# Attention output transposed straight into its packed tile, items taken in pairs, and a new planned order, in a one-core transformer block on Trainium2

## The chip, the core and the metric

The kernel runs on one core of one Trainium2 chip. The time is the device time of the whole program in microseconds; three runs of the kernel before took 803.64, 804.56 and 806.51 us, median 804.56. Profiles come from one profiled execution each.

## What is computed

The reference is one adaLN-conditioned transformer block on `x` of 2048 rows by 640 columns, in bfloat16:

```python
mod = (_silu(c) @ w_mod).reshape(c.shape[0], 6, 1, -1)      # sa, ca, ga, sb, cb, gb
h = _layernorm(x, axis=-1) * (1 + ca) + sa
x = x + ga * _A_ref(h, A_wqkv, A_wo)    # 32 heads of width 20, softmax over all 2048 keys
h = _layernorm(x, axis=-1) * (1 + cb) + sb
x = x + gb * _B_ref(h, B_w_gate, B_w_up, B_w_down)          # (h @ gate) * (h @ up) @ down, width 1536
```

## The kernel before

**The work.** The queries are cut into seven chunks (`CHUNKS`): one of 512 and six of 256. The 32 heads are eight groups of four; the four heads of a group sit in the four 32-row strips of a tile. A chunk and a group make an **item** (57 of them; the last of the last chunk is cut into two halves of 128 queries). Each item is cut into **units**: 512 columns of scores of one head in one PSUM bank (one block of 128 keys by 512 queries, or two by 256). There are 2048 units.

**Two ways to the exponential.** Most units go to ScalarE, two units, 1024 columns, to one exponential (`fexp`, line 1561) into a ring `PP` of eight double slots. The rest go to VectorE in **quads** of four units: it reads the scores from PSUM as integers (`fp1`, line 1585) and makes two terms by bit operations (lines 1617 and 1625) and one product, on POOL in four pieces (line 1637) or on VectorE (line 1622). `QUADS` says how many quads each item has, 107 in all: 428 units by VectorE, 1620 by ScalarE in 810 exponentials. A quad's units are multiplied with V twice, once for each term.

**The order.** `build_kernel` makes `Task` objects with durations, dependencies, priorities and buffers (`Slots`), and `Sched` plays them on a model of the engines; the order that comes out is written as five fixed instruction streams (`emit_program`, line 356). TensorE's next piece is chosen in `pick_pe` (line 2396): scores first when ScalarE has a bank free (`setA` and `setB`, two banks each), score work for VectorE attached to them (`d_attach`, line 2351), then products with V (`pv_issue`, line 2207), then pieces of projections and of the second half of the block (`pick_x`, line 2294). Constants such as `SEM`, `PE_DRAIN`, `ACT_LAT` and a table `STAGE` for each item set delays and thresholds. On SP's queue the transfers are taken by priority as soon as they are ready in the model.

**The end of an item** (`item_end_tasks`, line 1707). The products with V of one item gather in one bank of the pool `G` (four banks), 21 rows per head: a row of sums and 20 of output. Then VectorE transposes 32x32 blocks into `OT` (`t1`, line 1717), takes reciprocals of the sums (`t2`, line 1723), the normalisation goes to POOL or, for the last item of a chunk, to VectorE (`f3`, line 1725), and VectorE transposes back into `OcT` (`t4`, line 1734). Now each head's 20 rows stand in a strip of 32, and DMAs on SP's queue copy them to packed rows of `Ocp`, four or five for an item (line 1746):

```python
return e.dma_start(Ocp[r0:r0 + nr, slot, b5, qo:qo + n],
                   OcT[32 * s + 1 + ro:32 * s + 1 + ro + nr, cell["s"], 0:n])
```

The very last group has no copy; its `OcT` is multiplied directly with `wo7`, a small spread copy of the last rows of w_o.

**The second half** of a chunk (`suffix`, line 1773) runs beside the attention of the next chunk: out-projection from `Ocp` and `wo_sb` (`qf(320, ...)`), layernorm, transposes, gate and up with weights staged by DMA into `stg` (three buffers), a product (lines 1959 and 1966 for chunks of 256, one block of 128 hidden columns at a time, gate and up side by side in one bank), down-projection, and the output DMA (line 2071). The second half of the last chunk is the tail of the kernel. Early on the same SP queue carries the round trip of K and Q through DRAM (`packed_round`, line 1224: writes at line 1276, reads at 1289 and 1298).

## Time and profile before

| what | value |
|---|---|
| median of three runs | 804.56 us |
| span of the profiled execution | 803.8 us |
| first exponential starts, last ends | 16.35 us, 775.87 us |
| VectorE, ScalarE, TensorE busy, 16 to 109 us | 76.24, 85.71, 90.75 of 93 us |
| the same, 109 to 776 us | 595.30, 665.17, 661.40 of 667 us |
| the same, 776 to 804 us | 15.53, 4.05, 24.92 of 28 us |
| issues of copies from `OcT` to `Ocp` on SP | 248, median 714 ns |

How to read the lines below: a group's row has the source line, the engine, the operation, output and input with their shapes, the count after x, then busy time and mean duration, then the idle time ahead of it with what ended it. A row of the timeline has start, length, engine, line and count of instructions run together. In a table of windows each engine has its busy time and, in brackets, its count; behind them stand TensorE's granted clock, the share of DMA and GB/s. A waits row has total, times and longest. PEld is TensorE's weight load, which carries the wait of the matmul behind it; SPq is SP's DMA queue.

### The profile page before, as it was taken

The page shows a single profiled execution, that of the slowest core. Times are in us where ns is not written, and L with a number is a line of the kernel's source. Part 1 is how long each engine was busy: PE and PEld are TensorE (multiplying, and loading weights), DVE is VectorE, ACT ScalarE, POOL GpSimd, SP SyncE. Part 2 cuts the span into 40 slices and gives each one's busy share as a digit, 9 for nine tenths or more (in the row PEclk, how much of TensorE's full clock was granted, in tenths as well). Part 3 has the DMA queues.
Part 4 walks back from the last instruction along what each step waited for, and adds up shares of the span by engine and source line. Part 5 has one row for each costly group of instructions (what it writes and reads, how often), then busy time and mean ns, then how long its engine had stood idle before and what let it go on. Part 6 is the DMA issues. An engine that isn't in the chain of part 4 may idle for free.

```text
span 803.8 us, 37761 instructions
## 1 busy us (share of the span) xinstructions
PE 790.4 (98%) x16595; PEld 380.6 (47%) x16595; DVE 697.8 (87%) x1401; ACT 764.8 (95%) x847; POOL 386.0 (48%) x396
## 2 busy tenths in 40 slices
PE   8999999999999999999999999999999999999998
PEld 4433433333244434445555455555555555555567
DVE  7978788799989999988999999999899988898754
ACT  6899899999999999999999999999999999999961
POOL 3347455654366565763444443545534554455300
PEclk9999999999999999999999999999999999999999
DMA  9733212212341532120032404231540254414420
GB/s 297 243 113 91 62 43 64 61 33 76 92 109 50 167 88 52 35 55 13 24 81 65 95 16 112 57 73 39 121 89 15 54 118 94 98 37 106 92 68 18
DMA packets 154314, 64.66 MB, mean 80 GB/s; under 512 B 116951, under 2 KB 154151, under 8 KB 154151
## 3 DMA queue, kind: packets, MB, share of 16 engines
q1 hardware_dynamic: 153223, 61.10, 30.0%
q8 instruction: 132, 2.16, 1.1%
q10 hardware_dynamic: 928, 1.15, 0.5%
q14 instruction: 31, 0.25, 0.1%
HBM read 50.63 MB, written 8.99 MB: 74 GB/s over the span
## 4 chain that ended last, share of the span: by engine, by line
PE 77%; ACT 14%; DVE 5%; issue 2%; DMA 1%; SPq 1%; POOL 0%; DVEq 0%; ACTq 0%
PE ps_all L1524 26%; PE ps_all L970 21%; PE ps_all L2192 19%; ACT PP L1561 14%; PE ps_all L1230 4%; PE ps_all L966 3%; DVE DB L1585 2%; PE ps_all L1889 1%; PE ps_all L1166 1%; PE ps_all L1127 1%; DVE DSS L1617 1%; PE ps_all L2523 0%; DVE DSS L1625 0%; DMA QT<-q_rows 0%; PE ps_all L991 0%
## 5 line engine op out<-in xcount | busy, mean ns | idle before, releaser
L1561 ACT ACTIVATE PP<-ps_all 128x1024 bf16<-128x1024 f32 x810 | 748.5, 1090 | 6.7 <-PE ps_all L1524 4.8
L1637 POOL TENSOR_TENSOR DSS<-DB,DSS 128x512 bf16<-128x512 bf16 x268 | 305.0, 1157 | 290.6 <-DVE DSS L1625 254.2
L1585 DVE TENSOR_SCALAR DB<-ps_all 128x512 int16<-128x512 f32 x428 | 285.5, 681 | 50.5 <-PE ps_all L1524 48.0
L1524 PE MATMUL ps_all<-QT,KT 32*128 32x256 bf16 (+2 forms) x3648 | 319.4, 287 | 4.5 <-DMA QT<-q_rows 0.8
L1524 PEld LDWEIGHTS ps_all<-QT,KT 32*128 32x128 bf16 x3648 | 93.9, 92 | 204.1 <-ACT PP L1561 141.5
L2192 PE MATMUL ps_all<-PP,Vf 128*32 128x256 bf16 (+2 forms) x2892 | 163.6, 291 | 0.5 <-DVE KPB L1242 0.3
L970 PE MATMUL ps_all<-h2T,stg 128*32 128x256 bf16 (+2 forms) x2716 | 122.9, 281 | 0.3 <-DVE DB L1585 0.2
L2192 PEld LDWEIGHTS ps_all<-PP,Vf 128*32 128x32 bf16 (+1 forms) x2892 | 54.5, 94 | 76.4 <-issue 67.6
L2192 PE MATMUL ps_all<-DSS,Vf 128*32 128x256 bf16 (+1 forms) x1512 | 88.7, 291 | 0.0
L1617 DVE TENSOR_SCALAR DSS<-DB 128x2048 int16<-128x2048 int16 x107 | 77.2, 722 | 0.8
L970 PEld LDWEIGHTS ps_all<-h2T,stg 128*32 128x32 bf16 x2716 | 61.6, 96 | 26.9 <-issue 22.0
L1625 DVE TENSOR_SCALAR DSS<-DB 128x2048 int16<-128x2048 int16 x107 | 73.2, 684 | 0.8 <-PE ps_all L2192 0.8
L970 PE MATMUL ps_all<-wd,hprod 128*32 128x320 bf16 (+1 forms) x1404 | 61.0, 277 | 0.0
L1725 POOL TENSOR_TENSOR OTn<-OT,invT 128x256 bf16<-128x256 f32 (+1 forms) x49 | 35.3, 721 | 37.7 <-DVE invT L1723 37.5
L1622 DVE TENSOR_TENSOR DSS<-DB,DSS 128x2048 bf16<-128x2048 bf16 x40 | 51.5, 1287 | 0.0
L2192 PEld LDWEIGHTS ps_all<-DSS,Vf 128*32 128x32 bf16 x1512 | 36.5, 95 | 20.9 <-issue 12.4
L970 PE MATMUL ps_all<-wV,hT 128*32 128x160 bf16 x1280 | 38.9, 236 | 0.9 <-DVE DB L1585 0.3
L970 PEld LDWEIGHTS ps_all<-wd,hprod 128*32 128x32 bf16 x1404 | 31.2, 96 | 14.2 <-issue 10.8
L1717 DVE STREAM_TRANSPOSE OT<-ps_all 128x256 f32<-128x256 f32 (+2 forms) x57 | 27.1, 475 | 8.8 <-PE ps_all L2192 8.5
L1230 PE MATMUL ps_all<-hT,wk 128*32 128x512 bf16 x360 | 32.3, 382 | 0.0
L970 PEld LDWEIGHTS ps_all<-wV,hT 128*32 128x32 bf16 x1280 | 24.6, 97 | 15.9 <-issue 8.2
L1230 PE MATMUL ps_all<-hT,wq 128*32 128x512 bf16 x375 | 31.3, 382 | 0.6 <-DVE OT L1717 0.6
(133 smaller groups left out, 556.1 us busy)
## 6 DMA issues: line engine op xcount, KB each, us to landing
stg<-in_B_w_gate_dram SPq DMA_DIRECT2D x74, 160.0 KB
stg<-in_B_w_up_dram SPq DMA_DIRECT2D x74, 160.0 KB
KT<-k_rows SPq DMA_DIRECT2D x112, 32.0 KB
QT<-q_rows SPq DMA_DIRECT2D x48, 64.0 KB
Ocp<-OcT SPq DMA_DIRECT2D x164, 10.0 KB
wm<-in_w_mod_dram SPq DMA_DIRECT2D x3, 800.0 KB
x<-in_A_x_dram SPq DMA_DIRECT2D x7, 320.0 KB
k_rows<-KPA SPq DMA_DIRECT2D x16, 128.0 KB
```

Of the source, the lines that this page charges most:

```text
L970: return lambda e, b: e.matmul(ps[32 * x:32 * x + 32, b, c0 + o:c0 + o + w], lhs()[:, 32 * x:32 * x + 32], rhs() if w == n else rhs()[:, o ...
L1230: f = [lambda e, b_, k=k, x=x: e.matmul(ps[x:x + min(32, w - x), b_, :], wx[:, k, r0 + x:r0 + min(x + 32, w)], hT[tc][:, k, :], tile_posit ...
L1524: ems.append(lambda e, i=i, kt=kt: e.matmul(dstf()[:, i * u.n:(i + 1) * u.n], KT[32 * u.s:32 * u.s + 32, u.j, kt * 128:(kt + 1) * 128], QT ...
L1561: return e.activation(PPs[g % 2][:, cellp["p"], 0:nu * 512], ps[:, b0:b0 + nu, :].rearrange("p b c -> p (b c)"), AFT.Exp, scale=ESCALE)
L1585: return e.tensor_scalar(DBl[st_["slot"]][:, x * 512:(x + 1) * 512], bank(cell["b"]), EBIAS, 0.0, op0=ALU.add, op1=ALU.max)
L1617: return e.tensor_scalar(DSl[st_["ss"][0]][:, :], DBl[st_["slot"]][:, :], 0x7F, 0x3F00, op0=ALU.bitwise_and, op1=ALU.bitwise_or)
L1622: return e.tensor_tensor(d, DBl[st_["slot"]][:, :].bitcast(BF16), d, ALU.mult)
L1625: return e.tensor_scalar(DSl[st_["ss"][1]][:, :], DBl[st_["slot"]][:, :], 0x7F80, 2, op0=ALU.bitwise_and, op1=ALU.bitwise_or)
L1637: return e.tensor_tensor(d, DBl[st_["slot"]][:, x * w:x * w + w].bitcast(BF16), d, ALU.mult)
L1717: t1 = Task("dve", n * 1.1 + 70, lambda e: e.transpose(OT[:, 0:n], ps[:, item_info[it]["bank"], 0:n].rearrange("p (b q r) -> p b r q", q=3 ...
L1725: f3 = lambda e: e.tensor_tensor(OTn[:, 0:n].rearrange("p (b c r) -> p b r c", c=32, r=2), OT[:, 0:n].rearrange("p (b r c) -> p b r c", c= ...
L2192: ems.append(lambda e, i=i, kt=kt, stt=stt, stp=stp: e.matmul(ps[32 * s:32 * s + mc, bk, 0:u.n], Vf[:, (kt * H + 4 * u.j + s) * VW:(kt * H ...
```

## The change

The two transposes stay, but the way between them is new. The normalisation (`f3`) writes only the 20 output columns of a head, without the sums and the filling, into a tile `OTn` that holds all eight groups of a chunk side by side: 160 columns, which are five blocks of 32. As soon as a block of 32 is full, one VectorE transpose (`t4`) writes it straight into `Ocp`. `OcT`, `wo7` and the copies on SP's queue are gone. The rows of w_o stand in another order for it, so w_o is loaded by 48 DMAs of 4 to 20 rows instead of one large and four small.

Two items of 256 queries that follow each other share one PSUM bank and one first transpose of 512 columns (`PAIRS`): 34 first transposes instead of 57. Gate and up of a chunk of 256 take two blocks at once, gate in one bank and up in another (`GU2`), with two more staging buffers (`MORE`). `PP` is a ring of 16 single slots, and which units a score visit takes is decided when it is planned (`visit`), looking up to six units ahead for another head.

`QUADS` has 109 quads, so ScalarE has 1612 units. The planner gets corrections to its delays (`LAT_X`, `REL_X`, `V_X`, `S_X`), and nearly all constants and the table `STAGE` have new values; those are not shown. Options that are new in the code but off (`DUAL`, `V2`, `INTER` and `KDJ` at 1, the three-bank visits before the end) are not shown either.

```diff
+T3_NS = 2.2
+LAT_X = {("dve", "pe"): 35.0, ("dve", "pool"): 60.0, ("pes", "dve"): 28.0, ("pe", "dve"): -15.0, ("pe", "act"): -30.0,
+         ("pes", "act"): -15.0, ("act", "pe"): -80.0, ("act", "dve"): -180.0}
+REL_X = {"dve": 100.0, "act": -75.0}
+V_X = 8.0
+S_X = {4: -8.0, 6: 3.0, 8: 9.0}
+
+
+def seen_at(d, eng):
+    if d.nbytes:
+        return d.done + SEM
+    return d.done + SEM + LAT_X.get(("pes" if d.mode == "S" else d.eng, eng), 0.0)
...
-QUADS = ((0, 4, 3, 3, 3, 4, 4, 4), (2, 2, 1, 2, 2, 2, 1, 2), (2, 2, 1, 2, 2, 2, 1, 2), (2, 2, 1, 2, 2, 2, 1, 2), (2, 2, 1, 2, 2, 2, 1, 2), (2, 2, 1, 2, 2, 2, 1, 2), (2, 1, 2, 2, 2, 1, 2, 0))
+QUADS = ((0, 5, 3, 3, 3, 4, 3, 4), (2, 2, 2, 2, 2, 2, 1, 2), (1, 2, 1, 2, 2, 2, 1, 2), (1, 3, 1, 1, 2, 2, 1, 3), (2, 2, 1, 2, 3, 1, 1, 2), (2, 2, 1, 2, 2, 1, 2, 3), (2, 1, 2, 1, 1, 2, 4, 3))
...
+MORE = 2
...
+GU2 = 1
...
+PAIRS = 1
+LOOK = 6
+NPP = 16
...
+    PP = alloc("PP", [128, NPP, 512], BF16)
...
-    OTn = alloc("OTn", [128, 512], BF16)
-    NOC = 2
-    OcT = alloc("OcT", [128, NOC, 512], BF16)
     oc_off = region(2 * KD * 512 * 2)
-    Ocp = at("Ocp", [128, 2, KD, 512], BF16, oc_off)
+    assert all(n <= 256 for (_, n) in CHUNKS[1::2])
+    Ocp = [at("Ocp", [128, KD, 512], BF16, oc_off), at("Ocp", [128, KD, 256], BF16, oc_off + KD * 512 * 2)]
...
+    OTn = at("OTn", [128, 8, NSET * DH, 2], BF16, otn_off)
...
+    kpb_off = region(2 * KD * 128 * 2)
+    KPB = at("KPB", [128, 2, 512], BF16, kpb_off)
+    for off in (oc_off + KD * 768 * 2, kpb_off)[:MORE]:
+        stg.append(at("stg", [128, 2, KD, 128], BF16, off))
...
+    lead, second = {}, {}
+    for it in range(len(items) - 1):
+        if PAIRS and items[it][1] % 2 == 0 and spans[it] == spans[it + 1] and spans[it][1] == 256:
+            lead[it + 1] = it
+            second[it] = it + 1
+
+    def own(it):
+        return lead.get(it, it)
+
+    def coff(it):
+        return 256 if it in lead else 0
...
-    d_wo = [dma("sp", 128 * KD * D * 2, lambda e: e.dma_start(wo_sb[:, :, :], wov[:, :, :]), [d_wm[3][0]], prio=10)]
-    d_w7 = [dma("sp", DH * D * 2, lambda e, s=s: e.dma_start(
-        wo7[32 * s + 1:32 * s + 1 + DH, :], wov[48 + DH * s:48 + DH * s + DH, KD - 1, :]), [z_w7, d_wm[4][0]], prio=10.2) for s in range(4)]
+    d_wo = [[] for _ in range(KD)]
+    for j in range(NSET):
+        i0 = DH * j
+        while i0 < DH * j + DH:
+            i1 = min(DH * j + DH, i0 // 32 * 32 + 32)
+            for x in range(4):
+                def fwo(e, x=x, i0=i0, i1=i1, j=j):
+                    r0 = 4 * DH * j + DH * x + i0 - DH * j
+                    p0 = 32 * x + i0 % 32
+                    return e.dma_start(wo_sb[p0:p0 + i1 - i0, i0 // 32, :], A_wo[r0:r0 + i1 - i0, :])
+                d_wo[i0 // 32].append(dma("sp", (i1 - i0) * D * 2, fwo, [d_wm[3][0]], prio=10 + .01 * i0))
+            i0 = i1
...
         t2 = dve(155, lambda e: e.reciprocal(invT[:, 0:nb32].unsqueeze(2),
                                             OT[:, 0:n].rearrange("p (b c) -> p b c", c=32)[:, :, 0:1]), [t1], prio=pe_)
-        f3 = lambda e: e.tensor_tensor(
-            OTn[:, 0:n].rearrange("p (b c r) -> p b r c", c=32, r=2),
-            OT[:, 0:n].rearrange("p (b r c) -> p b r c", c=32, r=2),
-            invT[:, 0:nb32].rearrange("p (b r) -> p b r", r=2).unsqueeze(3).to_broadcast([128, nb32 // 2, 2, 32]), ALU.mult)
-        direct = j == NSET - 1 and ci == NC - 1
+        g0, gn = qo // 64, nq_ // 64
+
+        def f3(x):
+            return lambda e: e.tensor_tensor(
+                OTn[:, g0:g0 + gn, DH * (j + x):DH * (j + x) + DH, :].rearrange("p b c r -> p b r c"),
+                OT[:, nq_ * x:nq_ * x + nq_].rearrange("p (b r c) -> p b r c", c=32, r=2)[:, :, :, 1:1 + DH],
+                invT[:, 2 * gn * x:2 * gn * (x + 1)].rearrange("p (b r) -> p b r", r=2).unsqueeze(3).to_broadcast(
+                    [128, gn, 2, DH]), ALU.mult)
+        ds = [t2] + [y for x in range(nm) for b in range(DH * (j + x) // 32, (DH * (j + x) + DH - 1) // 32 + 1)
+                     for y in ot_read.get((ci - 1, b), [])]
+        nv = nq_ * DH // 32
         if pooled:
-            t3 = pool(n * 2.2 + 200, f3, [t2], prio=0)
+            t3 = pool(nm * (nv * T3_NS + 150), [f3(x) for x in range(nm)], ds, prio=0)
         else:
-            t3 = dvl(sb_cost(n, 1.04), f3, [t2], prio=pe_)
-        t4 = dve(n * .55 + 65, lambda e: e.transpose(OcT[:, cell["s"], 0:n].bitcast(F32), OTn[:, 0:n].bitcast(F32)), [t3],
-                 prio=pe_)
-        pcs = [] if direct else oc_pieces(j)
-        t4.acq = [(sOcT, "s", max(1, len(pcs)))]
-
-        def on4(task):
-            cell["s"] = task.slots["s"]
-            sOT.done(0, task)
-        t4.on_start = on4
-        dms = []
-        for (b5, s, r0, nr, ro) in pcs:
-            def f(e, b5=b5, s=s, r0=r0, nr=nr, ro=ro):
-                return e.dma_start(Ocp[r0:r0 + nr, slot, b5, qo:qo + n],
-                                   OcT[32 * s + 1 + ro:32 * s + 1 + ro + nr, cell["s"], 0:n])
-            dps = [t4] + ([z_oc[slot]] if b5 == KD - 1 else []) + (z_tail[ci] if b5 == KD - 1 else [])
+            t3 = dvl(nm * sb_cost(nv, 1.04), [f3(x) for x in range(nm)], ds, prio=pe_)
+        t3.on_start = lambda task: sOT.done(0, task)
+        b0, b1 = (DH * j) // 32 if j else 0, DH * (j + nm) // 32
+        tls = range(qo // 128, (qo + nq_) // 128)
+        if b1 > b0:
+            nbk = b1 - b0
+            dps = [t3]
+            if ci == 0:
+                dps += [x for l in q_zero.values() for x in l] + [z_oc]
             if ci >= 2:
                 dps += oc_free[ci - 2]
             else:
                 dps += [x for l in tr_last.values() for x in l]
-            t = dma("sp", nr * n * 2, f, dps, prio=1.05 if j >= NSET - 2 else 2, dur=720.0)
-            t.firm = ci == NC - 1 and it >= len(items) - 2
-            t.on_start = lambda task: sOcT.done(cell["s"], task)
-            dms.append(t)
-        tls = range(qo // 128, (qo + n) // 128)
-        for x in tls:
-            oc_ready.setdefault((ci, x), []).extend(dms)
-            if direct:
-                oc_ready[(ci, x)] += z_tail[ci]
-                oc_ready[(ci, x)].append(t4)
-                oc_last[x] = (cell, 128 * x - qo)
+
+            def f4(e):
+                o = Ocp[slot][:, b0:b1, qo:qo + nq_].bitcast(F32).rearrange("p k (b c) -> p k b c", c=32)
+                i = OTn[:, g0:g0 + gn, 32 * b0:32 * b1, :].rearrange("p b (k c) r -> p k b (c r)", c=32).bitcast(F32)
+                if nbk == 1:
+                    o, i = o[:, 0], i[:, 0]
+                return e.transpose(o, i)
+            t4 = dve(nq_ * nbk * .55 + 65, f4, dps, prio=pe_)
+            for b in range(b0, b1):
+                ot_read.setdefault((ci, b), []).append(t4)
+            for x in tls:
+                oc_ready.setdefault((ci, x), []).append(t4)
...
+            if n <= 256 and GU2:
+                two.append((wbuf, dm))
+                if fc % 2 == 0:
+                    continue
+                gs = fc // 2 % 2
+                pair, two = two, []
+                for w_ in range(2):
+                    mms = []
+                    for x in range(2):
+                        for k in range(KD):
+                            f = qf(n, lambda k=k, cell=pair[x][0][w_]: cell["t"][:, k, :], lambda k=k: h2T[:, k, 0:n],
+                                   k == 0, k == KD - 1, x * n)
+                            mms.append((X(n), f))
+                    if w_ == 0:
+                        def after(r, gs=gs):
+                            f = lambda e: e.tensor_copy(gsb[:, gs, 0:2 * n], ps[:, r.b["b"], 0:2 * n])
+                            fa = lambda e: e.copy(gsb[:, gs, 0:2 * n], ps[:, r.b["b"], 0:2 * n])
+                            ds = [r.last] + ([g_use[gs]] if gs in g_use else []) + sc_use
+                            return [evac(2 * n, ps_cost(2 * n), f, fa, ds)]
+                    else:
+                        def after(r, gs=gs, fc=fc, eg=eg):
+                            f = lambda e: e.tensor_tensor(
+                                hprod[:, fc - 1:fc + 1, 0:n], ps[:, r.b["b"], 0:2 * n].rearrange("p (a b) -> p a b", a=2),
+                                gsb[:, gs, 0:2 * n].rearrange("p (a b) -> p a b", a=2), ALU.mult)
+                            return [dve(ps_cost(2 * n), f, [r.last, eg] + (hp_free if alt else bd.get("hp", []) + proj_early + kv_last), prio=1)]
+                    r = Round(mms, t_h2 + [pair[0][1][w_], pair[1][1][w_]] + sfx_done.get("ul", []), after, pr(),
+                              gate=gate(2 * KD * n), name=f"{'gu'[w_]}{ci}.{fc}")
+                    if w_ == 0:
+                        eg = r.evac[0]
+                    else:
+                        g_use[gs] = r.evac[0]
+                        hp.append(r.evac[0])
+                        u_last.append(r.last)
+
+                    def off(task, w_=w_, pair=pair):
+                        for x in range(2):
+                            sStg[w_].done(pair[x][0][w_]["i"], task)
+                    r.last.on_start = off
...
+    def visit(t):
+        a = setS.avail()
+        if a is None or a[0] > t:
+            return False
+        ap = pvstate["ap"]
+        k = setS.free[a[1]][0]
...
+        w = 2 if pick is not None or not size3(k) else 3
+        seen = {pick.s} if pick is not None else set()
+        for x in range(ap, min(NA, ap + LOOK)):
+            u = ubuf[x]
+            if len(us) < w and u.s not in seen and (x < ap + 2 or all(d.done is not None and d.done + SEM <= t for d in first_deps(u))):
+                seen.add(u.s)
+                us.append(u)
+        if ap < NA and not us:
+            us = [ubuf[ap]]
+        for u in us:
+            ubuf.remove(u)
+        ubuf[ap:ap] = us
+        pvstate["ap"] = ap = ap + len(us)
+        nu = len(us)
...
+            def fexp(e, nu=nu, b0=b0, cellp=cellp):
+                p = cellp["p"]
+                o = PP[:, p[0]:p[-1] + 1:(p[1] - p[0] if nu > 1 else 1), :]
+                return e.activation(o, ps[:, b0:b0 + nu, :], AFT.Exp, scale=ESCALE)
+            ta = Task("act", nu * 512 / 1.2 + 52.0, fexp, [ts], prio=pvstate["sidx"], name=f"E{pvstate['sidx']}")
+            ta.acq = [(ppr, "p", 1, nu)]
```

747 lines of the change are left out of this document (462 added, 285 removed).

## The prediction

> **What bounds the kernel now.** I read the page first (span, busy time, the chain that ended last, the exponential's group), then ScalarE's timeline, then the waits of the steady part, then the chain of the one visible hole.
>
> ```profile
> span 803.8 us, 37761 instructions
> ...
> PE 790.4 (98%) x16595; PEld 380.6 (47%) x16595; DVE 697.8 (87%) x1401; ACT 764.8 (95%) x847; POOL 386.0 (48%) x396
> ...
> PE 77%; ACT 14%; DVE 5%; issue 2%; DMA 1%; SPq 1%; POOL 0%; DVEq 0%; ACTq 0%
> ...
> L1561 ACT ACTIVATE PP<-ps_all 128x1024 bf16<-128x1024 f32 x810 | 748.5, 1090 | 6.7 <-PE ps_all L1524 4.8
> ```
>
> The profiled execution lasted 803.8 us; the median of the runs is 804.56, so I add 0.76 us to whatever the sum gives. Three engines look nearly full, and records that overlap hide the idle time: an exponential's record is 1090 ns long, yet the next one starts earlier. ScalarE's timeline tells the true pitch.
>
> ```profile
> 410.43 17.53 ACT L1561 ACTIVATE PP<-ps_all 128x1024 bf16<-128x1024 f32 x19
> ...
> 425.80 2.16 ACT L1561 ACTIVATE PP<-ps_all 128x1024 bf16<-128x1024 f32 x2
> ```
>
> Both rows end with the same exponential, so 17 starts lie between them: (425.80 - 410.43)/17 = 0.904 us. That is the floor for 1024 columns. Now the whole stretch, row by row:
>
> ```profile
> 16.35 7.51 ACT L1561 ACTIVATE PP<-ps_all 128x1024 bf16<-128x1024 f32 x8
> ...
> 108.67 124.80 ACT L1561 ACTIVATE PP<-ps_all 128x1024 bf16<-128x1024 f32 x135
> 233.72 76.14 ACT L1561 ACTIVATE PP<-ps_all 128x1024 bf16<-128x1024 f32 x82 [0.26 <-PE ps_all L1524]
> 310.05 64.15 ACT L1561 ACTIVATE PP<-ps_all 128x1024 bf16<-128x1024 f32 x69 [0.19 <-PE ps_all L1524]
> 374.56 262.18 ACT L1561 ACTIVATE PP<-ps_all 128x1024 bf16<-128x1024 f32 x284 [0.36 <-PE ps_all L1524]
> 637.04 138.83 ACT L1561 ACTIVATE PP<-ps_all 128x1024 bf16<-128x1024 f32 x151 [0.29 <-PE ps_all L1524]
> ```
>
> The exponentials run from 16.35 to 775.87 us (637.04 + 138.83), 759.5 us. At the floor 810 of them take 732.2, so **27.3 us are holes**. From 108.67 on there are 721 in 667.2 us: 651.8 at the floor and **15.4 of small holes**. The other 11.9 lie in the first 92 us. So the time is 16.4 us before the first exponential, 732.2 of ScalarE at its floor, 27.3 of holes and 27.9 of tail. ScalarE sets the pace; what can be won is fewer exponentials, fewer holes, a shorter tail.
>
> ```profile
> PEld ps_all L1524 <- ACT PP L1561: 118.5, 421, 0.8
> ```
>
> That is the longest wait of a busy engine between 120 and 770 us, and the next row is the steady part in the table of windows:
>
> ```profile
> 109.00:776.00 667.00, 661.40 (x14456) 314.68 (x14451) 595.30 (x1144) 665.17 (x721) 331.69 (x323) 1.00 0.30 72
> ```
>
> In the steady part TensorE's score loads waited 118.5 us for ScalarE to free a bank: it comes early more often than late, and VectorE, third number, is 89% full.
>
> **The change, part by part.** *(a) Work moved.* The table of quads goes from 107 to 109. A quad is four units of 512 score columns, and ScalarE takes two units in one exponential: 810 becomes 806, -4 x 0.904 = **-3.6 us**. TensorE pays 8 more second passes on balance.
>
> ```profile
> 407.46 0.78 PE ps_all L2192 x24
> ```
>
> Eight passes are 16 matmuls of 256 columns; at 0.78/24 each that is 0.5 us of TensorE, beside its 118.5 us of waits. The Trainium skill (VectorE: DVE Perf Modes, section on the TRN2 errata) gives ScalarE 172 cycles plus one per column from PSUM, an estimated 997 ns for 1024 columns; part (a) would be -4.0 us by it. The pitch of 904 ns contradicts it as a spacing, since 810 x 0.997 is more than the whole span.
>
> *(b) No copies on SP's queue.* The transposed output was copied into `Ocp` by 20-row DMAs; now a VectorE transpose writes `Ocp`. The hole at 84 to 94 us shows what the copies held up.
>
> ```profile
> 87.61 0.76 SPq L1746
> ...
> 89.88 0.72 SPq L1746
> 90.60 0.06 issue
> ...
> 90.71 3.51 DMA QT<-q_rows
> 94.22 0.09 issue
> 94.31 0.45 PE ps_all L1524 x4
> ```
>
> The table of windows has the same place:
>
> ```profile
> 80.00:100.00 20.00, 18.93 (x375) 8.51 (x375) 14.32 (x32) 17.30 (x19) 10.18 (x9) 0.92 0.26 68
> ```
>
> Scores wait for a Q tile, whose read stands on SP behind four copy issues, 87.61 to 90.60 = 3.0 us. ScalarE is busy 17.30 of 20 us there, and the granted clock falls to 0.92. Without the copies the read goes 3.0 us earlier; what is late next is the 3.51 us transfer itself, so I take **-3.0 us** and not the whole hole. Against it, one load of w_o plus four small ones become 48 small ones on the same queue.
>
> ```profile
> L970 PE MATMUL ps_all<-wo,Ocp x656: 232/299/311, 228.8 to 699.7; 128*32 128x320 bf16 x116, 128*32 128x160 bf16 x48
> ...
> L1497 DVE TENSOR_TENSOR wo<-wo,gab x5: 474/477/479, 87.6 to 90.0; 128x640 bf16<-128x640 bf16 x5
> L1493 SPq DMA_DIRECT2D wo<-in_A_wo_dram x4: 327/396/1384, 33.1 to 36.2; - x4
> ```
>
> 48 x 0.396 = 19.0 us of SP. They rank behind K and Q reads; w_o was loaded by 37 us, scaled at 87.6 and first multiplied at 228.8, so SP's idle stretches can take them: 0. If that cover is gone they cost up to 19.0 (rival 4).
>
> *(c) VectorE's load.* Two items of 256 queries now share a PSUM bank, so one 512-column transpose serves both; gate and up are evacuated two blocks at a time; and the last transpose goes by 32-row blocks.
>
> ```profile
> L1585 DVE TENSOR_SCALAR DB<-ps_all 128x512 int16<-128x512 f32 x428 | 285.5, 681 | 50.5 <-PE ps_all L1524 48.0
> ...
> L1617 DVE TENSOR_SCALAR DSS<-DB 128x2048 int16<-128x2048 int16 x107 | 77.2, 722 | 0.8
> L1625 DVE TENSOR_SCALAR DSS<-DB 128x2048 int16<-128x2048 int16 x107 | 73.2, 684 | 0.8 <-PE ps_all L2192 0.8
> ...
> L1622 DVE TENSOR_TENSOR DSS<-DB,DSS 128x2048 bf16<-128x2048 bf16 x40 | 51.5, 1287 | 0.0
> ...
> L1959 DVE CAST gsb<-ps_all 128x256 bf16<-128x256 f32 x60 | 24.6, 412 | 4.7 <-PE ps_all L970 4.6
> ...
> L1717 DVE STREAM_TRANSPOSE OT<-ps_all 128x256 f32<-128x256 f32 x47 | 20.8, 442 | 4.8 <-PE ps_all L2192 4.7
> ...
> L1734 DVE STREAM_TRANSPOSE OcT<-OTn 128x128 f32<-128x128 f32 x47 | 14.2, 301 | 1.5 <-POOL OTn L1725 1.5
> ...
> L1986 DVE CAST gsb<-ps_all 128x512 bf16<-128x512 f32 x12 | 8.1, 674 | 0.5 <-PE ps_all L970 0.5
> ...
> L1717 DVE STREAM_TRANSPOSE OT<-ps_all 128x512 f32<-128x512 f32 x8 | 5.7, 712 | 1.4 <-PE ps_all L2192 1.3
> ...
> L1734 DVE STREAM_TRANSPOSE OcT<-OTn 128x256 f32<-128x256 f32 x8 | 3.5, 433 | 0.0
> ```
>
> First transpose: 47 x 0.442 + 8 x 0.712 = 26.5 becomes 31 x 0.712 + 0.442 = 22.5, -4.0. Last transpose: 47 x 0.301 + 8 x 0.433 = 17.6 becomes 10 wide (five in chunk 0, one each in chunks 1 to 5) x 0.433 + 19 narrow x 0.301 = 10.0, -7.6; its strided output has no row, so from -12.6 (half the price) to +2.4 (double). Gate and up: 60 casts at 0.412 and as many products, taken at the same price, become 30 each at 0.674: 49.4 to 40.4, -9.0. Two quads add 8 x 0.681 + 2 x (0.722 + 0.684) + 0.37 x 2 x 1.287 = 9.2. Together about **-11 us of VectorE**, in 667 us where it is 89% full. The normalisation on POOL shrinks too (20 of 32 columns), but POOL is 48% busy: 0.
>
> What do 11 us and a new order buy of the 15.4 us of small holes? No row shows it. Bounds: -15.4 (all close) and +17 (rival 3). I take **-6**, nearer to none than to all, because the chain of waits is 77% TensorE and TensorE's load does not fall. The holes of the first 92 us other than (b) I leave, 0, from -8.9 (11.9 - 3.0, all of it) to as much again: they lie among the projections, whose order changes but not their amount.
>
> *(d) Added waits.* A pair is transposed when both items are done, so one of four spare banks is held twice as long but opened half as often. A gate round needs two weight tiles; two more staging buffers come with it. A normalisation on POOL waits for the previous chunk's transposes, with the quads' products queued behind it; those transposes are about 100 us old by then. 0 each.
>
> *(e) Tail.* The first half's out-projection waited for the last copies.
>
> ```profile
> 769.17 0.73 SPq L1746 DMA_DIRECT2D Ocp<-OcT  x1
> ...
> 770.51 0.24 DVE L1734 STREAM_TRANSPOSE OcT<-OTn 128x64 f32<-128x64 f32 x1
> ...
> 771.72 0.45 PE L966 MATMUL ps_all<-wo,Ocp 128*128 128x320 bf16 x2
> ```
>
> The direct transpose ended at 770.75, the matmul began at 771.72, after the copy issued at 769.17. That saves up to 0.9 us; a sixth block per half also goes. I take **-1.0 us**; the tail behind it is the same work.
>
> **Sum:** -3.6 - 3.0 - 6.0 - 1.0 = -13.6; 803.8 - 13.6 + 0.76 = **791.0 us**.
>
> **Rivals.** *1. Freed VectorE time buys nothing*, since TensorE is 98% busy and its order, not VectorE, makes the holes. Then 803.8 - 3.6 - 3.0 - 1.0 + 0.76 = 797.0. For it: the 77%. Against it: 118.5 us of TensorE waiting.
>
> *2. The measured delays fit*, and 13 of the 15.4 close: 784.0. For it: stretches of 17 exponentials at 0.904 exist. Against it: the holes sit at many different causes.
>
> *3. Slower: TensorE waits in line.* The planner's new figures let it count a ScalarE result 80 ns sooner at TensorE. If the chip is not that quick, a score load is queued too early, and everything behind it on TensorE's in-order queue stands. Place: the 421 waits above; price 421 x 0.08 = 33.7 us, of which half, 16.9, would fall where ScalarE has no bank in hand: 803.8 - 7.6 + 16.9 + 0.76 = 813.9. It decides once the waits grow by 15.2 us, half of which eats the other 7.6. Against it: today's waits average 0.28 us, so loads already come early and the correction may just be true.
>
> *4. The 48 loads stand ahead of the Q and K reads.* All 19.0 us in front of the read at 90.71: 803.8 - 3.6 - 6.0 - 1.0 + 16.0 + 0.76 = 810.0; slower once 34 of them stand there (13.6/0.396). The Trainium skill (DMA: Bandwidth & Descriptors, section Bandwidth) speaks against splitting: under 64 KB, transfers are ruled by descriptors. No run here shows 48 such loads in a row.
>
> **How the numbers follow.** Forecast 0.53; rival 1 0.18; rival 2 0.16; rival 3 0.08; rival 4 0.05. Range 782 to 803: it takes in rivals 1 and 2 and leaves out 3, 4 and the far end of 2. A measurement of this kernel tells about 0.3% (2.4 us) from no change. Faster by more: 0.87; within: 0.04 (milder forms of 3 and 4); slower: 0.09.
>
> **What would show it.** 806 exponentials; no copies into `Ocp`; the hole at 84 to 94 us shorter and the clock at 1.00 there; VectorE's busy time near 686; holes from 108 us on near 9 us; last exponential to end near 27 us. More than 806 exponentials (a visit that finds one unit only), last transposes far above 0.43 us, or SP still on the chain at 90 us would make the prediction wrong.

## The result, and the profile after

The change made the kernel slower: 809.13 us (median of five, 806.97 to 810.62) against 804.26 us (median of five, 803.64 to 806.51); the ratio is 1.0054, 95% interval 1.0033 to 1.0075. 791.0 had been forecast, with a range up to 803. The profiled execution took 807.3 us of span, 3.5 more than before, and its time is 809.13: each run's time lies about 1.8 us above its span.

The page after: span, busy time, the chain that ended last, the exponential's group.

```profile
span 807.3 us, 37537 instructions
...
PE 793.3 (98%) x16648; PEld 383.4 (47%) x16648; DVE 682.9 (85%) x1276; ACT 759.1 (94%) x847; POOL 401.6 (50%) x416
...
PE 59%; ACT 30%; issue 5%; DVE 3%; SPq 2%; DMA 1%; ACTq 0%; DVEq 0%
...
L2656 ACT ACTIVATE PP<-ps_all 128x1024 bf16<-128x1024 f32 x806 | 740.9, 1197 | 11.9 <-PE ps_all L2356 6.8
```

806 exponentials, as counted; VectorE 14.9 us less busy, more than the 11 forecast. ScalarE's timeline gives the stretches; the last column is the idle time before a row and what ended it.

```profile
16.84 7.39 ACT L2656 ACTIVATE PP<-ps_all 128x1024 bf16<-128x1024 f32 x8
...
38.16 21.32 ACT L2656 ACTIVATE PP<-ps_all 128x1024 bf16<-128x1024 f32 x23
61.18 1.02 ACT L2656 ACTIVATE PP<-ps_all 128x1024 bf16<-128x1024 f32 x1 [1.69 <-PE ps_all L1679]
...
85.71 6.52 ACT L2656 ACTIVATE PP<-ps_all 128x1024 bf16<-128x1024 f32 x7 [1.20 <-PE ps_all L2356]
94.04 1.94 ACT L2656 ACTIVATE PP<-ps_all 128x1024 bf16<-128x1024 f32 x2 [1.81 <-PE ps_all L2356]
96.99 59.71 ACT L2656 ACTIVATE PP<-ps_all 128x1024 bf16<-128x1024 f32 x65 [1.01 <-PE ps_all L2356]
...
529.79 245.96 ACT L2656 ACTIVATE PP<-ps_all 128x1024 bf16<-128x1024 f32 x268 [2.83 <-PE ps_all L2356]
```

By the prediction's own reckoning (floor 0.904 us for each exponential; early holes up to 96.99 us here, where 71 have run, and up to 105.94 before, where 86 have):

| part | before | after | difference | forecast |
|---|---|---|---|---|
| first exponential starts | 16.35 | 16.84 | +0.5 | 0 |
| exponentials at the floor | 732.2 | 728.6 | -3.6 | -3.6 |
| holes, early | 11.8 | 16.0 | +4.2 | -3.0 |
| holes, steady | 15.4 | 14.3 | -1.1 | -6.0 |
| tail behind the last exponential | 27.9 | 31.55 | +3.6 | -1.0 |

The four exponentials saved are there. Three other terms have to be explained: early, steady, tail. The floor itself is too low: ScalarE needs 0.917 us for an exponential of 1024 columns, which is worked out behind the run exp960. By it the exponentials are 742.8 and 739.1 us, the early holes 10.7 and 15.0, the steady ones 6.0 and 4.8. The differences move by 0.1 us at most, but only 6.0 us of steady holes were there to be closed, and not 15.4. The holes of the runs below are by 0.904, like the table, so that they can be compared with it.

### The profile page after: what moved, and what is told of

Read it like the earlier page. It is cut to its first block, busy times and chain, and to the rows that moved or that the text cites. A ratio compares the mean times of both kernels' runs of the same rounds, so it can differ in the third digit from the quotient of the medians.

```text
span 807.3 us, 37537 instructions
## 1 busy us (share of the span) xinstructions
PE 793.3 (98%) x16648; PEld 383.4 (47%) x16648; DVE 682.9 (85%) x1276; ACT 759.1 (94%) x847; POOL 401.6 (50%) x416
## 4 chain that ended last, share of the span: by engine, by line
PE 59%; ACT 30%; issue 5%; DVE 3%; SPq 2%; DMA 1%; ACTq 0%; DVEq 0%
ACT PP L2656 30%; PE ps_all L1679 20%; PE ps_all L1093 17%; PE ps_all L2356 14%; PE ps_all L1089 3%; PE ps_all L1353 2%; DVE DB L1706 1%; SPq L1648 1%; PE ps_all L2000 1%; PE ps_all L2819 1%; PE ps_all L1289 1%; PE ps_all L1250 0%; DMA x<-in_A_x_dram 0%; SPq L1412 0%; PE ps_all L1114 0%
## 5 line engine op out<-in xcount | busy, mean ns | idle before, releaser
L2656 ACT ACTIVATE PP<-ps_all 128x1024 bf16<-128x1024 f32 x806 | 740.9, 1197 | 11.9 <-PE ps_all L2356 6.8
L1762 POOL TENSOR_TENSOR DSS<-DB,DSS 128x512 bf16<-128x512 bf16 x296 | 335.1, 1156 | 302.1 <-DVE DSS L1750 249.7
L1706 DVE TENSOR_SCALAR DB<-ps_all 128x512 int16<-128x512 f32 x436 | 292.0, 684 | 70.6 <-PE ps_all L1679 68.8
L2356 PE MATMUL ps_all<-PP,Vf 128*32 128x256 bf16 (+3 forms) x2876 | 163.1, 291 | 0.0
L2356 PE MATMUL ps_all<-DSS,Vf 128*32 128x256 bf16 (+3 forms) x1544 | 90.9, 290 | 0.0
L1093 PEld LDWEIGHTS ps_all<-h2T,stg 128*32 128x32 bf16 x2808 | 62.9, 96 | 27.7 <-issue 24.1
L2356 PEld LDWEIGHTS ps_all<-DSS,Vf 128*32 128x32 bf16 (+1 forms) x1544 | 39.6, 96 | 16.8 <-issue 11.0
L1747 DVE TENSOR_TENSOR DSS<-DB,DSS 128x2048 bf16<-128x2048 bf16 x35 | 43.2, 1235 | 0.0
L1843 POOL TENSOR_TENSOR OTn<-OT,invT 128x160 bf16<-128x160 f32 (+1 forms) x44 | 22.0, 519 | 22.7 <-DVE invT L1838 22.5
L1353 PE MATMUL ps_all<-hT,wk 128*32 128x512 bf16 (+1 forms) x360 | 33.1, 385 | 0.1
L1093 PE MATMUL ps_all<-wo,Ocp 128*32 128x320 bf16 (+1 forms) x660 | 31.5, 281 | 0.3 <-DVE xck L1941 0.2
```

The lines of the kernel that those rows point to most:

```text
L1093: return lambda e, b: e.matmul(ps[32 * x:32 * x + 32, b, c0 + o:c0 + o + w], lhs()[:, 32 * x:32 * x + 32], rhs() if w == n else rhs()[:, o ...
L1353: f = [lambda e, b_, k=k, x=x: e.matmul(ps[x:x + min(32, w - x), b_, :], wx[:, k, r0 + x:r0 + min(x + 32, w)], hT[tc][:, k, :], tile_posit ...
L1706: return e.tensor_scalar(DBl[st_["slot"]][:, x * 512:(x + 1) * 512], bank(cell["b"]), EBIAS, 0.0, op0=ALU.add, op1=ALU.max)
L1747: return e.tensor_tensor(d, DBl[st_["slot"]][:, :].bitcast(BF16), d, ALU.mult)
L1762: return e.tensor_tensor(d, DBl[st_["slot"]][:, x * w:x * w + w].bitcast(BF16), d, ALU.mult)
L1843: return lambda e: e.tensor_tensor(OTn[:, g0:g0 + gn, DH * (j + x):DH * (j + x) + DH, :].rearrange("p b c r -> p b r c"), OT[:, nq_ * x:nq ...
```

## The experiments

Each ratio is to the kernel before, run beside it. "Order kept" means that every engine gets its instructions in the planned order of the changed kernel, edited only as the diff says.

### Early: SP's queue

```diff
 # wo5_same_order, on the finished order
-for t in d_wo[k]: 48 loads of 8 to 20 rows, at their 48 places
+one.emits = [lambda e, k=k: e.dma_start(wo_sb[:, k, :], A_wo[128 * k:128 * k + 128, :])]
 # wo_late, on the finished order
+put(lst, wo[:32], 94.5e3); put(lst, wo[32:], 170e3); t_wo[k] at 206e3 + 2500 * k
```

> The changed kernel with its planned order kept on every engine; only the 48 small loads of w_o are replaced by five, one for each block of 128 rows, each at the place of the first small one of its block, and the other 43 are taken out of SP's queue. The permutation of the rows is left out by this. Theory A (the small loads stand ahead of the K reads on SP's queue): the wait for a KT read at 58.5 to 64 us goes, the granted clock at 60 to 80 us comes back to 1.00, the holes before 108 us fall from 16.0 to about 13, and the time falls by 2 to 3 us, to about 806.5. Rival (the projections on TensorE set the early holes, and what the loads cost is hidden or given back before 108 us): the last early exponential stands where it stood, within 0.8 us, and the time stays at 808 to 810.

Measured: 805.88 us, ratio 1.0007 (0.9992 to 1.0021).

> The changed kernel whole, with the 48 small loads of w_o moved on SP's queue: 32 of them behind the reads that end at 95 us, where SP idles until 111 us, the other 16 to the idle stretch at 170 us; VectorE's five scalings of w_o go from 93 to about 206 us and further, ahead of the first output projection at 230 us. Nothing else moves. Theory A (what cost time was their place ahead of the K reads, not their number): no wait for a KT read at 58 us, holes before 97 us near 12.7 as with five loads, time 805.5 to 806.5, that is 3 us below the change and level with before. Rival (48 small loads cost time wherever they stand, as DMA traffic or behind the K reads of the next set): over 807.5, with a wait for a KT or QT read at 112 to 130 or 175 to 185 us.

Measured: 806.08 us, ratio 1.0021 (1.0010 to 1.0033). SP's timeline of the changed kernel shows what both remove:

```profile
44.39 3.43 SPq L1648 DMA_DIRECT2D wo<-in_A_wo_dram  x7
...
52.78 0.42 SPq L1399 DMA_DIRECT2D k_rows<-KPA  x1
53.25 3.11 SPq L1648 DMA_DIRECT2D wo<-in_A_wo_dram  x7
56.40 2.69 SPq L1412 DMA_DIRECT2D KT<-k_rows  x4
```

and its chain of the hole, in order of time, what follows from it:

```profile
56.75 1.14 SPq L1412
57.89 0.43 issue
58.32 0.31 SPq L1412
58.63 0.06 issue
58.69 1.87 DMA KT<-k_rows
60.55 0.20 issue
60.75 0.40 PE ps_all L1679 x4
```

Seven loads of w_o, 0.44 us each, stand in front of four K reads. Eleven more, from 44.39 us on, stand in front of the write of K at 52.78 that these reads fetch, and SP is never idle for more than 0.1 us in between. The scores wait for the last read, and from 60 to 80 us the granted clock is 0.91. In wo_late the same write and reads are issued 3.2 and 4.5 us earlier:

```profile
49.54 0.34 SPq L1399 DMA_DIRECT2D k_rows<-KPA  x1
51.94 1.72 SPq L1412 DMA_DIRECT2D KT<-k_rows  x4
```

and ScalarE's timeline there runs through:

```profile
38.28 28.66 ACT L2656 ACTIVATE PP<-ps_all 128x1024 bf16<-128x1024 f32 x31
67.52 13.86 ACT L2656 ACTIVATE PP<-ps_all 128x1024 bf16<-128x1024 f32 x15 [0.58 <-PE ps_all L1679]
```

The early holes fall from 16.0 to 12.6 us, and the time by 3.05 us from median to median (the ratio to before from 1.0054 to 1.0021). Theory A holds for both: it was the place of the loads, not their number. The spread shrank too: eleven runs of wo_late lie between 806.00 and 806.75 us, five of the change between 806.97 and 810.62, so the wait for the K read is probably also what varied from run to run.

### Early: what holds ScalarE at 80 to 100 us

```diff
 # before_copies_behind: the kernel before, SP's queue only
-4 copies Ocp<-OcT, 2 reads QT<-q_rows
+2 reads QT<-q_rows, 4 copies Ocp<-OcT
 # early_less: as wo5_same_order, and for V, K, Q and w_mod rounds planned at 76 to 95 us
+    if not t.deps and id(t) not in used: t.emits = []
```

> The kernel before, its order kept, but for four copies into Ocp on SP's queue, issued from 87.61 to 90.60 us: they stand behind the two QT reads that followed them. Theory of the prediction's step (b) (the copies cost what the read is late, 3.0 us): the QT reads issue up to 3.0 us earlier, at 88 to 88.5 at the earliest since they read what was written 2 to 3 us before, the hole at 84 to 100 us shrinks by 2 to 3 us, the granted clock at 95 to 100 us comes up from 0.69, and the time falls by 2 to 3 us. Rival (TensorE's projections and VectorE hold the scores there anyway, as in the changed kernel, which has 4 us of holes at 80 to 95 us with SP clear): time within 1 us of the kernel before.

Measured: 804.19 us, ratio 0.9997 (0.9985 to 1.0009). In the profiled execution the reads went 2.0 us earlier (88.67 instead of 90.71) and the early holes fell from 11.8 to 9.3 us, and yet the median does not move. The trace that the prediction was made from was an execution with a large hole: its span is 803.8, and with 1.8 us on top it stands at 805.6, while the median of seventeen runs in this comparison is 803.97. Fifteen of the seventeen had a granted clock of 1.000 over the whole span; the profiled execution had 0.998, with the dip to 0.92 at 80 to 100 us. And the profiled execution with the reads ahead, 802.77 us, is one of the two fastest of its twelve. The read's lateness is partly chance; a median does not hold 3.0 us of it.

> As the kernel with five loads of w_o, same order; left out besides are the middle matmuls of the projections that the plan puts at 76 to 95 us (rounds of V, K and Q and the two vectors of w_mod), about 4.9 us of TensorE. Theory C (with SP's queue clear, TensorE's projections are what ScalarE waits for at 80 to 95 us, so the 3.0 us that the prediction took for the copies were covered by TensorE work): the three holes there, 4 us in all, shrink to about 1, and the time falls by 2.5 to 4 us below the 805.9 of the kernel with five loads. Rival (the products wait there for VectorE or POOL results): holes and time within 1 us.

Measured: 806.71 us, ratio 1.0028 (1.0016 to 1.0040), not under 805.88: the rival. The windows of 85 to 95 us, first of wo5_same_order, then of early_less (columns: length, busy time and count of PE, PEld, DVE, ACT, POOL, clock, DMA share, GB/s):

```profile
85.00:95.00 10.00, 10.00 (x249) 5.80 (x245) 9.96 (x21) 7.20 (x9) 3.25 (x3) 1.00 0.24 70
```

```profile
85.00:95.00 10.00, 8.14 (x123) 3.18 (x123) 9.97 (x22) 7.25 (x9) 3.06 (x3) 1.00 0.22 60
```

TensorE got 1.9 us of air and ScalarE none: VectorE is full in both. In the changed kernel this place has SP clear, a clock of 1.00 (80 to 100 us), and still 4 us of holes. With the five loads TensorE and VectorE are both at 10 of 10 us there, so they are the likely next limits. wo_late moved five scalings of w_o out of VectorE's way (VectorE 8.36 of 10 us) and the holes did not change either, so neither alone decides; what holds ScalarE there stays open.

### Steady: whose time is it

```diff
 # dve1920 (the same in fx and fe); full width at a buffer's first use
-e.tensor_scalar(DSl[..][:, :], DBl[..][:, :], 0x7F, 0x3F00, ...)
+e.tensor_scalar(DSl[..][:, 0:1920], DBl[..][:, 0:1920], 0x7F, 0x3F00, ...)
 # exp960; full width at a buffer's first use
-return e.activation(o, ps[:, b0:b0 + nu, :], AFT.Exp, scale=ESCALE)
+return e.activation(o, ps[:, b0:b0 + nu, 0:480], AFT.Exp, scale=ESCALE)
```

> The changed kernel with its planned order; VectorE's three operations on 2048 columns of each quad (two bit operations, and the product where VectorE makes it) work on 1920 columns, except at the first use of each buffer. 128 of a quad's 2048 columns are left out. VectorE's busy time falls by about 12 us (218 operations by 0.042 and 35 by 0.075), as much again as the change freed. The prediction's step (freed VectorE time closes steady holes, 6 us for 11): the steady holes fall from 14 to about 8 and the time by 5 to 6 us. Rival (VectorE's time is not what the holes wait for): holes within 1.5 us of 14, time within 2 us.

Measured: 807.80 us, ratio 1.0038 (1.0019 to 1.0057), VectorE 9.0 us less busy (12 had been expected). Its longest row of exponentials:

```profile
528.47 245.96 ACT L2666 ACTIVATE PP<-ps_all 128x1024 bf16<-128x1024 f32 x268 [2.75 <-PE ps_all L2366]
```

268 exponentials in 245.96 us, to the hundredth what the change has: the rival. At this order, VectorE's time buys nothing. The spans differ by 1.3 us (806.0 and 807.3), and 1.2 of it are early holes, 14.8 us here.

> The changed kernel with its planned order; each exponential works on 480 of 512 columns of each of its two units, except at the first use of each buffer, so 1 of 16 columns is left out. By the pitch of 0.904 us, if it is all columns, an exponential is 0.053 us shorter at the floor (64 columns at 0.83 ns): 806 of them 43 us. If ScalarE alone sets the pace, the time falls by 35 to 43 us, to 766 to 774. If TensorE sets it as well (it waits in line for ScalarE, but has little time to spare), the time falls by less than 20 us and ScalarE's holes grow by what is missing. If TensorE alone sets it, within 5 us.

Measured: 799.36 us, ratio 0.9934 (0.9913 to 0.9956): 9.8 us under the change, not 43. Its chain, and two of its rows:

```profile
PE 86%; DVE 9%; SPq 2%; ACT 1%; issue 1%; DMA 1%; DVEq 0%; ACTq 0%
```

```profile
93.87 1.83 ACT L2659 ACTIVATE PP<-ps_all 128x960 bf16<-128x960 f32 x2 [2.07 <-PE ps_all L2357]
...
523.42 181.16 ACT L2659 ACTIVATE PP<-ps_all 128x960 bf16<-128x960 f32 x200 [3.06 <-PE ps_all L2357]
```

Two back to back take 1.83 us, and a record is 0.975 us on the mean, so ScalarE's own pitch for 960 columns is 0.86; but 200 of them run at (181.16 - 0.975)/199 = 0.905 us, and ScalarE's share of the chain falls from 30% to 1%. ScalarE now waits, and the chain is 86% TensorE's: with what TensorE has to do for one exponential, it needs 0.905 us in this order. That is the second of the three cases expected.

What does ScalarE need at full width? Not the 0.904 us of the prediction. In its row of 19 exponentials of the kernel before, from 410.43 us on, the first one is

```profile
410.43 1.03 ACT L1561 ACTIVATE PP<-ps_all 128x1024 bf16<-128x1024 f32 x1
```

so the 18 behind it end (17.53 - 1.03)/18 = **0.917 us** apart. The starts lie 0.904 apart only because the records grow, from 1.03 to 1.26 us: each is started a little earlier behind one that still runs. The ends tell the pace. The changed kernel's rows give the same, (245.96 - 1.02)/267 and (59.71 - 1.02)/64, both 0.917. It is ScalarE's own pace and not TensorE's, since TensorE can do 0.905 in the same order.

So in the steady part of the changed kernel ScalarE sets the pace, and TensorE stands 0.012 us behind it. Over 735 exponentials that is 9 us, an estimate from the two pitches, close to the 9.8 us that this run won. It is also why dve1920 won nothing in its long row: ScalarE ran there at its own pace already. The page's chain puts 59% down to TensorE and 30% to ScalarE; with two engines this close, those shares do not tell which one sets the pace.

> The kernel with the 48 loads moved (wo_late), its order kept; added are 408 small matmuls, by issuing the middle matmuls of the down-projections of chunks 2 and 3 twice, so that their sums count twice: 11 us of TensorE (0.027 us each, the plan's figure) between 545 and 640 us. Theory F (TensorE is full: the 172 us for which its score loads wait for ScalarE are streaming time of the matmuls ahead and no spare time): the time grows by 8 to 11 us. Rival (the prediction's reading: ScalarE sets the pace and TensorE has 100 us to spare): the time grows by less than 2 us.

> The same addition in the kernel before: 420 small matmuls, 11 us of TensorE between 534 and 630 us. Theory F (TensorE was full before the change already, so four exponentials less and 11 us less of VectorE could not shorten the steady part): the time grows by 8 to 11 us. Rival (the 118.5 us of waits that the prediction read as room): less than 2 us.

```diff
+if t.name[:3] in ("dn2", "dn3") and not t.deps and id(t) not in used:
+    t.emits = t.emits * 2
```

Measured: 816.41 us in the changed kernel, 10.3 above wo_late, ratio 1.0148 (1.0133 to 1.0163); 815.79 us in the kernel before, ratio 1.0136 (1.0119 to 1.0153), 10.9 us more. The first lines of the two pages, changed kernel first:

```profile
PE 801.9 (98%) x17056; PEld 393.1 (48%) x17056; DVE 683.9 (84%) x1276; ACT 762.6 (94%) x847; POOL 402.3 (49%) x416
```

```profile
PE 802.3 (98%) x17015; PEld 391.4 (48%) x17015; DVE 698.5 (86%) x1401; ACT 768.1 (94%) x847; POOL 385.0 (47%) x396
```

Some 11 us more for TensorE (by the plan's 0.027 us a matmul) cost some 11 us: 10.3/408 = 25 ns a matmul after the change, 10.9/420 = 26 ns before it. **TensorE was all but full already.** Its busy time grew with the span and its share stayed at 98%. The waits of the score loads for ScalarE (118.5 us before; after the change, over the same stretch, the next row) are no spare time. The likely reason is that the matmuls ahead of a waiting load still stream; by its records TensorE's matmuls are busy 98% of the span. Between 545 and 650 us these waits fell from 24.1 us in wo_late to 10.0 in tensor_more, and the time grew all the same.

```profile
PEld ps_all L1679 <- ACT PP L2656: 166.1, 633, 0.7
```

The Trainium skill (Perfetto Trace Analysis, section Identifying the Most-Contended Engine) calls matmul busy time a poor measure and points to the rate of useful matmul work and the busy share of weight loads instead. The weight loads here are at 47%, which would leave room; the added matmuls say that there is next to none. Here the measurement decides against that reading.

```diff
+if t.name[:3] in ("dn0", "dn1", "dn2", "dn3", "dn4") and not t.deps and id(t) not in used:
+    t.emits = []
```

> As the kernel with five loads of w_o, same order; left out besides are the middle matmuls of the down-projections of chunks 0 to 4, about 33 us of TensorE between 370 and 725 us. Theory D (in the steady part TensorE needs as long for one exponential's share of work as ScalarE, 0.905 against 0.904 us; their unequal waits make most of the small holes): the mean pitch at 530 to 725 us falls from 0.917 to 0.908 or less, and the time by 3 to 5 us to about 802. Rival (ScalarE's own pitch is 0.917 on the mean, nothing waits): pitch within 0.003, time within 1.5 us. The stall of 3.0 us at 523 us is in the order and stays by both if VectorE makes it.

Measured: 828.16 us, ratio 1.0279 (1.0243 to 1.0316); a miss by both theories. Two windows:

```profile
380.00:400.00 20.00, 18.57 (x231) 6.26 (x226) 11.26 (x20) 17.59 (x20) 6.37 (x8) 0.59 0.05 18
400.00:420.00 20.00, 19.36 (x230) 6.45 (x224) 12.13 (x22) 18.14 (x19) 9.19 (x9) 0.50 0.03 10
```

With the work taken out, the granted clock (third number from the end) falls to 0.59 and 0.50, and the matmuls that are left take longer than what was saved. So its time tests neither theory. About the pitch the rival was right, as the ends showed above: 0.917 us is ScalarE's own, and theory D's 0.904 is not.

### The tail

```diff
 # tail_less_wd: the change, behind the last exponential
+if t.name[:4] == "dn5." and t.start > t_end and not t.deps and id(t) not in used: t.emits = []
 # tail_fix: wo_late, and by hand
+2 last POOL pieces of the last quad: no wait for VectorE's normalisation of the item behind
+TensorE: that quad's second pass one sum earlier; output projection ahead of dn5.0's end and dn5.1
+VectorE: that item's transposes ahead of the evacuations of dn5
 # tail_both: tail_fix and tail_less_wd's edit
```

> The changed kernel with its planned order; left out are those matmuls of the previous chunk's down-projection that the plan puts behind the last exponential (some 35 groups of four, 0.04 us a matmul, about 5 us of TensorE), except the first and the last of each sum. Theory B (at the last exponential TensorE has more work left than before the change, and this backlog is the tail): the tail of 31.55 us falls by 3 to 5 us, to 27 to 28.5, and the time to about 805. Rival (the tail is the chain of the last item: its late quads, transposes, normalisation, output projection; TensorE's other work only fills its gaps): the tail stays within 1 us, and TensorE shows 4 us of idle time there. Half of it, if both matter.

Measured: 808.25 us, ratio 1.0045 (1.0029 to 1.0060); tail 31.48 us. TensorE now waits, where it had waited for nothing:

```profile
778.91 2.62 PE L1089 MATMUL ps_all<-wo,Ocp 128*128 128x320 bf16 x18 [1.00 <-DVE Ocp L1873]
...
783.33 0.45 PE L1978 MATMUL ps_all<-ident,xn2c 128*128 128x128 bf16 x5 [1.42 <-DVE xn2c L1965]
```

Theory B, left-over work alone, falls.

> The kernel with the 48 loads moved (wo_late), and the order of its last 45 us changed by hand: the last two quarters of the product that POOL makes for the last quad no longer wait for VectorE's normalisation of the item behind it, the second-pass matmuls of that quad stand one down-projection sum earlier on TensorE, VectorE transposes that item at once, and the first half's output projection stands ahead of the rest of the previous chunk's down-projection. Nothing is left out. Theory B2 (the tail is the chain from the last full item's late quads through its transposes to the output projection; TensorE's other work only fills): the output projection starts about 2 us earlier against the last exponential's end (1.7 us behind it in the change), the tail falls from 31.6 to 29 to 30 us and the time by 1.5 to 2.5 us below wo_late's 806.1. Rival (the second half's chain or TensorE's order ends last): tail within 0.7 us of 31.6.

Measured: 807.41 us, ratio 1.0044 (1.0030 to 1.0058); tail 31.77 us. The output projection did come earlier (0.06 us behind the last exponential's end instead of 1.7), and was worth nothing for the tail: the transposes of the normalised rows stood behind 81 small down-projection matmuls on TensorE.

```profile
775.39 2.62 PE L1089 MATMUL ps_all<-wo,Ocp 128*128 128x320 bf16 x18
...
778.79 3.03 PE L1093 MATMUL ps_all<-wd,hprodt 128*32 128x320 bf16 x81
...
781.76 0.45 PE L1978 MATMUL ps_all<-ident,xn2c 128*128 128x128 bf16 x5
```

Theory B2 alone falls as well. The run also has a cost of its own, told in the last section: the last exponentials come about 1.1 us later against the start of their row than in wo_late, which the tail does not hold, and the whole stands 1.3 us above wo_late's 806.08. tail_both has this cost too.

> The kernel with the hand-ordered tail (tail_fix), and left out besides are the middle matmuls of the previous chunk's down-projection behind the last exponential, about 4.8 us of TensorE. Each of the two alone left the tail at 31.5 to 31.8 us. Theory E (two limits of equal length stand side by side in the tail, TensorE's left-over work and the chain of the last item; either one alone buys nothing): together the tail falls by 2 to 3 us, to 29 to 29.8. Rival (a third thing ends last, such as the second half's chain): the tail stays within 0.7 us of 31.6.

Measured: 805.38 us, ratio 0.9999 (0.9984 to 1.0014), 2.0 below tail_fix and 0.7 below wo_late; tail 29.85 us against 31.77. The size just misses what was expected (29 to 29.8), but either edit alone had moved the tail by 0.2 us at most. So theory E holds: the left-over work of the previous chunk and the chain of the last item stand side by side, of nearly equal length. What keeps the tail 1.9 us above the 27.9 of the kernel before stays open.

### Two parts undone alone

```diff
 # quads_old
-QUADS = ((0, 5, 3, 3, 3, 4, 3, 4), (2, 2, 2, 2, 2, 2, 1, 2), ...)
+QUADS = ((0, 4, 3, 3, 3, 4, 4, 4), (2, 2, 1, 2, 2, 2, 1, 2), ...)
 # delays_old
-LAT_X = {("dve", "pe"): 35.0, ...}
+LAT_X = {}
```

> Part (a) undone alone: the changed kernel with the old table of quads, 810 exponentials; the planner makes a new order with all its other numbers unchanged. If the number of exponentials is what counts: 3.6 us more in the exponentials and the old, shorter tail (3.65 less), so 807 to 813. Rival (the planner's numbers fit one table only, and another table throws the order off): over 815, with the steady holes or the tail changed by more than 5 us.

Measured: 820.89 us, ratio 1.0209 (1.0191 to 1.0226); early holes 16.0, steady 13.0, tail 40.4 us. The rival: with the old table in the new numbers, TensorE still has 192 down-projection matmuls and 240 of gate and up of the previous chunk to do behind the last exponential.

> One part undone alone: the changed kernel with the eight measured delays between engines put to zero; the planner makes a new order with all its other numbers unchanged. If the measured delays are what made the mean pitch better (0.917 us at 530 to 725 us against 0.923 before): the pitch there goes back to 0.921 or more and the steady holes grow by 3 us or more. If the delays don't matter for the pitch: within 0.002 of 0.917 away from single stalls. The time itself says little, since the new order may hold stalls of its own: 810 to 830.

Measured: 826.85 us, ratio 1.0287 (1.0263 to 1.0310); early holes 19.9, steady 21.0, tail 38.6 us. The steady holes grew by 6.7 us, mostly in single stalls. The long rows, first with the old table, then with the delays at zero:

```profile
439.22 338.77 ACT L2656 ACTIVATE PP<-ps_all 128x1024 bf16<-128x1024 f32 x369 [0.25 <-PE ps_all L1679]
```

```profile
511.96 22.10 ACT L2655 ACTIVATE PP<-ps_all 128x1024 bf16<-128x1024 f32 x24 [3.62 <-PE ps_all L2355]
...
560.23 159.64 ACT L2655 ACTIVATE PP<-ps_all 128x1024 bf16<-128x1024 f32 x174 [0.35 <-PE ps_all L1678]
```

Pitches of (338.77 - 1.02)/368 = 0.918 and (159.64 - 1.02)/173 = 0.917 us, as in the change, 0.917, against 0.923 in the row of 284 exponentials before. 0.917 is ScalarE's own pace, so what the change took away are the small waits that lie in the 0.923, and neither the quads nor the measured delays were needed for it; which of the other parts did it (pairs, gate and up two blocks at a time, the new transposes, the other numbers) stays open. What both kernels show is how far one entry throws the whole order: 12 and 18 us.

No version here that does the whole work beats the kernel before: wo_late stays 0.2% above it, before_copies_behind is level.

## Why the prediction was wrong

**The step that failed first is the reading of the room.** "ScalarE sets the pace" holds in the steady part. "What can be won is fewer exponentials, fewer holes" was read with a floor 0.013 us too low: 0.904 is the distance of starts, ScalarE's pace is 0.917, so of the "15.4 of small holes" 9.4 are ScalarE at work. And the 118.5 us of waits that were read as room on TensorE are next to none: TensorE needs 0.905 us for each exponential's share, and almost each microsecond added to it came out as a microsecond. The page said so, 98%, with 77% of the chain. The sum then has three terms that came out otherwise: early (-3.0 forecast, +4.2 measured), steady (-6.0, -1.1) and tail (-1.0, +3.6).

**(a) Fewer exponentials, -3.6.** Count and size were right; with the loads moved, the last exponential ends at 772.84 instead of 775.87. But at that moment TensorE has more work left than before, see (e), and the tail took it back. That the one follows from the other is not shown: quads_old, with 810 exponentials, has still more left.

**(b) SP's queue, -3.0 and 0.** Both halves failed. The copies' 3.0 us came from one execution with a large hole, and with the copies behind the reads the median did not move. And "they rank behind K and Q reads" was wrong about the 48 loads: rank decides among what is ready, and a load that is issued while no read is ready still stands in front of what becomes ready next. Rival 4 named the mechanism; its price was 19.0 us for all 48 in front of one read, and the runs give about 3 for all 48, by the chain from the eighteen between 44.39 and 56.40.

**(c) VectorE's 11 us, holes -6.** VectorE was relieved of 14.9 us. The transposes and gate and up came out as computed, the last transposes into the packed tile for instance:

```profile
L1873 DVE STREAM_TRANSPOSE Ocp<-OTn 128x128 f32<-128x128 f32 x19 | 5.8, 304 | 1.0 <-POOL OTn L1843 1.0
...
L1873 DVE STREAM_TRANSPOSE Ocp<-OTn 128x256 f32<-128x256 f32 x10 | 4.4, 435 | 0.8 <-POOL OTn L1843 0.8
```

304 and 435 ns against 301 and 433 into the plain tile: the strided output, taken at the plain price between half and double, costs nothing. The two quads, 9.2 us in the sum, cost nothing: the groups of the quads' operations together fall by 0.7 us, because VectorE makes the product of 35 quads instead of 40. What failed is the exchange of VectorE time for holes: dve1920 took 9 us more and left the rows as they were. Of the 6.0 us of holes that there were, the change did close most: 0.006 us of pitch over some 720 exponentials, about 4 us. A stall of 3 us in front of 529.79 took most of it back. That stall is of the order, not of chance: dve1920 and exp960 have it too (2.75 and 3.06). TensorE's timeline of the changed kernel in front of it:

```profile
520.14 0.62 PE L2356 MATMUL ps_all<-PP,Vf 128*32 128x256 bf16 x16
...
528.43 0.73 PE L1093 MATMUL ps_all<-h2T,stg 128*32 128x256 bf16 x20 [0.39 <-DVE DB L1706]
...
529.29 0.62 PE L2356 MATMUL ps_all<-PP,Vf 128*32 128x256 bf16 x16
```

For 9 us no product with V reads `PP`; its sixteen slots, room for eight exponentials, fill, and ScalarE waits. The product stands behind scores and rounds of gate and up, the last of which waits 0.39 us for VectorE to read a bank.

**(d) Added waits, 0.** No experiment took one of them out alone, so this step stays untested.

**(e) Tail, -1.0.** "The tail behind it is the same work" failed. TensorE's rows behind the last scores (774.02 us), first and last of five:

```profile
774.35 1.13 PE L1093 MATMUL ps_all<-wd,hprodt 128*32 128x320 bf16 x28
...
782.38 0.59 PE L1093 MATMUL ps_all<-wd,hprodt 128*32 128x320 bf16 x12
```

In all 136 down-projection matmuls of the previous chunk are left there, where 48 were before; and the last full item, with four quads instead of two, released the output projection later: it starts 5.7 us later (777.43 against 771.72) and the first transposes of normalised rows behind it 3.0 us later (781.99 against 778.94). tail_fix, tail_less_wd and tail_both show that both hold the tail: neither alone shortens it, both together by 1.9 of the 3.6 us. That the four quads are to blame is argued and not shown, since with the old table the tail is longer still.

**The 0.76 us.** A run's time is 1.8 us above its span in every run here. So the 0.76 did not turn a span into a time: it put the sum on the median, and hid that the profiled execution was itself about 1 us slower than the median.

Of the rivals, the first was nearest for the steady part in what it forecast (freed VectorE time buys nothing), though not in its reason: ScalarE itself left little to win there. The fourth was nearest for the early part. Rival 2's small holes did close, but there were never 13 us of them, and delays_old has the same pitch without the measured delays. Rival 3's sign shows, 166.1 us of waits instead of 118.5, well past its point of 15.2 us, but the steady holes did not grow; such waits are no price.
